# An attention and two MoE layers on one core: the order of a planned kernel, drawn anew

## The chip, the cores and the metric

The kernel runs on one core of one Trainium2 chip. The metric is the device time of one execution in microseconds, the median of several runs. TensorE (PE) does the matmuls, VectorE (DVE), ScalarE (ACT) and GpSimd (POOL) the elementwise work, and SyncE (SP) issues most of the DMA transfers. Each engine executes its own queue of instructions in order and waits at semaphores for the others.

## What is computed

Four images of 576 positions and 8 heads go through an attention with two branches: one on positions pooled by four, repeated over the four, and one in which a position sees its three neighbours on each side. Their sum, 2304 tokens of width 512, goes through two layers of the form "matmul, activation, matmul" with 2048 hidden columns. The inputs q, k, v and three weights are multiplied by 8 beforehand.

```python
attn_out = _attn_ref(q, k, v)                 # pooled branch + local branch
x = attn_out.transpose(0, 2, 1, 3).reshape(B * S, H * D)
h = x @ moe_w_in                              # first MoE
x = (h * (1.0 / (1.0 + np.exp(-h)))) @ moe_w_out
h = x @ moe2_w_in                             # second MoE
P = a[0] + a[1] * h + a[2] * h**2 + a[3] * h**3
Q = 1.0 + np.abs(b[0]) * np.abs(h) + np.abs(b[1]) * h**2
out = (P / (Q + 1e-06)) @ moe2_w_out
```

Weights come as 64-bit floats and are turned on the chip into pairs of 32-bit numbers, a rounded high part and the rest (`hl`); activations are split in the same way (`xh` and `xl`, `gh` and `gl`), and each product is the sum of three matmuls.

## The kernel before

**Stages.** In the head, PE has attention of image 0 and dummy matmuls on `wz` (line 328). Then the first MoE runs in 80 steps, one for each of five blocks of tokens (512, 384, 512, 512 and 384) and sixteen groups of 128 hidden columns. A step has 12 matmuls into `hps` (line 914), an activation on ACT and DVE (lines 1077 to 1089), and 12 matmuls into `acc` (line 928). The steps of block 0 are cut in two: 8 groups, then all of block 1, then the other 8. Between the steps stand, in islands, the attention of images 1 to 3, and on ACT, DVE and POOL the converting of the weights. The second MoE comes last, in a loop with an order written out by hand.

**What is planned.** All that comes before the second MoE is a list of jobs, each with a cost for each engine, a due time, the jobs that it comes after, the buffers it takes and gives, and the bytes it moves (`size`). `Plan.run` (line 150) plays them through on five engines (P, V, A, G, and D for SP) and returns the jobs in the order of their starts; the kernel then emits its instructions in that order. What is left at run time of a planned time is thus the order on each engine's queue. Three things in it concern transfers:

- Backwards (lines 163 to 166): a job's due time is that of its user, less its cost; for a transfer also less its bytes over a rate, a latency (`DMA_LAT`) and `PRE`.
- Forwards (lines 247 to 250): all transfers share one `bus`. A transfer holds it for its bytes over a rate, and its users are ready `DMA_LAT` later. Lines 213 to 216 hold a transfer back while the bus is planned more than `BACKLOG` (4 us) ahead.
- A job's `margin` is added to the time at which its predecessors are done (line 192).

`settle` (line 125) runs the plan twice, first with guessed starts of the steps (from `HEAD` on, line 359), then with the planned ones, keeps the better, and shifts due times by random draws, one after another for each of eight `SEEDS` (line 139). The dummies in the head fill a share of 0.8 of the planned idle time of PE (lines 1116 to 1126).

**The jobs that the change speaks of.** `piece` (line 807) loads 512 KB of 64-bit weights into `raw` (line 819) and converts them in seven jobs: `c1` (line 827 on ACT, 825 on DVE) and `c2` (line 831, ACT) read `raw`, `c3` to `c5` follow on DVE (834, 838, 842), `c6` (line 376 or 372, in the helper `copy`) and `c7` (line 850) write the two parts. For the first MoE's output weights (`wo`) the parts are also stored as `wos` (line 889) and loaded again for later blocks (line 1052); those of the second MoE are stored as `w2s` (line 898) and loaded from line 960. Attention loads `kq` (line 428) and `vw` (line 632); DVE pools k and q from `kq` (line 438), PE makes local scores (647, 655) and coarse ones (522), ACT exponentials (672, 539), PE transposes (687, 557), ACT copies (`PT`, `up`, line 376), and PE multiplies by v (722, 572). A block's output leaves `acc` as `xe` (lines 376 and 374, from 937) and is stored by SP (947) or, added, by POOL (945). `TAIL`, `TAIL1` and `STAG` set how long ahead of a block's first step its pieces of x are due (line 768). `raw`, `wo`, `xe` and the converted parts share one ring of seven buffers, `buf`.

Of the kernel before, what the change touches and what calls it, by code (L numbers as in the profile page):

```python
# [38 lines left out]
NEG = -1e30  # L39


HEAD = 42000.0
PACE = 1.06
TAIL, STAG, STAG0 = 40000.0, 4000.0, 2000.0
TAIL1 = 18000.0
SAFE = 4000.0
PRE = 3000.0
MARGIN = 800.0
# [8 lines left out]
BACKLOG = 4000.0  # L57
EARLY = 50000.0
ROUNDS = 2
SEEDS = [1000021, 1000022, 1000050, 1000057, 1000130, 1000133, 1000381, 1000809]  # L60
EARLYB = 20000.0
GPREF = 1
ACC = 108.0
# [42 lines left out]
class Plan:  # L106
# [1 line left out]

    LAT, OWN = 200.0, 90.0
    SWITCH = {(False, True): 90.0, (True, False): 195.0, (True, True): 0.0, (False, False): 0.0}  # L110
    DMA_LAT = 2500.0
    DMA_RATE, DMA_FULL, DMA_SLOW = 400.0, 11500.0, 285.0

    def __init__(self):
        self.jobs, self.sizes, self.lends = [], {}, {}
# [9 lines left out]
    def settle(self, when, rounds):  # L125
# [8 lines left out]
        self.run(when)  # L134
        for seed in SEEDS:
            self.shake(seed)
# [13 lines left out]
    def run(self, when):  # L150
# [12 lines left out]
        for j in reversed(self.jobs):  # L163
            for d in j.after:
                d.t = min(d.t, j.t - self.LAT - min(d.cost.values()) -
                          (d.size / self.DMA_RATE + self.DMA_LAT + PRE if d.size else 0.0))
            j.wait = len(j.after)
            j.ready = 0.0
            for d in j.after:
                users.setdefault(id(d), []).append(j)  # L170
# [3 lines left out]
        port = 0.0  # L174
        bus = 0.0
# [3 lines left out]
        while events:  # L179
# [3 lines left out]
            while done and done[0][0] <= t:  # L183
                _, _, j = heapq.heappop(done)
# [13 lines left out]
            while again:  # L198
                again = False
                for j in pool:  # L200
# [43 lines left out]
                    if held and not (best == "G" and j.size):  # L244
                        port = free[best]
                    heapq.heappush(events, free[best])
                    if j.size:
                        bus = max(bus, free[best])
                        bus += j.size / (self.DMA_RATE if bus > self.DMA_FULL else self.DMA_SLOW)
                        j.end = bus + self.DMA_LAT  # L250
                    else:
                        j.end = free[best]
# [39 lines left out]
def tile_kernel(ctx, tc, kq, vp, vw_in, moe_w_in, moe_w_out, moe2_w_in, moe2_w_out, moe2_a, moe2_b, out):  # L292
# [50 lines left out]
    plan = Plan()  # L343
# [14 lines left out]
    first1 = [STEP1.index((0 if f < SPLIT else 1, f)) for f in range(NF)]  # L358
    guess, t = [], HEAD
    for j, f in STEP1:  # L360
# [3 lines left out]
    FAR = At(0, 1e9)  # L364
# [50 lines left out]
    def attention(b):  # L415
# [201 lines left out]
        for c in range(NCH):  # L617
# [147 lines left out]
            def end(jo, pO, b=b, c=c, n=n, xu=xu, ad=ad, hi=hi, lo=lo):  # L765
                ja = plan.add(f"A{b}{c}", d0, {"V": 2 * v_ns(2 * n)}, ad, after=[jo], give=[pO, upu])
                for j, *p, i in pieces[b * NCH + c]:
                    due = begin[j] - (TAIL1 if j == 1 else TAIL) - (STAG if j else STAG0) * (behind[j] - 1 - i)
                    if i == 0:
# [37 lines left out]
    def piece(name, due, src, dst, home, after=None):  # L807
# [4 lines left out]
        wu, iu = Unit("cw"), Unit("cr")  # L812
# [37 lines left out]
            eng(e).tensor_tensor(out=x["hl"][:, 1], in0=x["w"], in1=x["hl"][:, 0], op=ALU.subtract)  # L850

        j0 = plan.add(f"{name}.l", FAR, {"D": 60}, ld, take=[home], size=128 * 4096)
        j1 = plan.add(f"{name}.1", FAR, {"A": 570, "V": 430}, c1, after=[j0], take=[wu], port=True)
        j2 = plan.add(f"{name}.2", FAR, {"A": 570}, c2, after=[j0], take=[iu])
        j3 = plan.add(f"{name}.3", FAR, {"V": 430}, c3, after=[j1], port=True)
        j4 = plan.add(f"{name}.4", FAR, {"V": 620}, c4, after=[j2, j3], port=True)
        j5 = plan.add(f"{name}.5", FAR, {"V": 620}, c5, after=[j4], give=[iu], port=True)
# [25 lines left out]
    for f in range(NF):  # L883
        wi_job[f] = piece(f"I{f}", when[first1[f]], win_src(moe_w_in, f), lambda u, f=f: new_wi(f), Unit(f"w{f}"))
        u = wo_u[first1[f]] = Unit("buf")

        def keep(x, j, f=f, u=u):
            wos_job[f] = plan.add(f"S{f}", when[first1[f]], {"D": 60},
                                  lambda e: nc.sync.dma_start(out=wos[f], in_=x["hl"].bitcast(F32)),
                                  after=[j], give=[u], size=128 * 4096, early=1e9)  # L890
        wo_job[f] = piece(f"O{f}", when[first1[f]] + 6000, wout_src(moe_w_out, f), lambda u, f=f: new_wo(first1[f]), u, keep)
    for f in range(NF):
        for s, w in enumerate((moe2_w_in, moe2_w_out)):
            u = Unit("buf")

            def keep2(x, j, f=f, s=s, u=u):
                w2_job[f, s] = plan.add(f"W{f}{s}", when[-1], {"D": 60},
                                        lambda e: nc.sync.dma_start(out=w2s[s, f], in_=x["hl"].bitcast(F32)),
                                        after=[j], give=[u], size=128 * 4096, early=1e9)
            piece(f"{'IO'[s]}2.{f}", when[NF + SPLIT + round((2 * f + s) * (3 * NF - SPLIT) / 32)], (win_src, wout_src)[s](w, f),  # L900
                  lambda u: buf(u, "cvo"), u, keep2)
# [298 lines left out]
    for s in range(ns + LAG2):  # L1200
        if s < ns:
            j, f = STEP2[s]
# [88 lines left out]
```

## Time and profile before

| | us |
|---|---|
| median of 3 runs | 908.48 |
| lowest, highest | 907.67, 908.97 |
| the profiled execution | 909.08 |
| its span, first to last instruction | 907.3 |

A row of the page's first part gives an engine's busy time, its share of the span and its instructions. A row of a table by stage has the window, its length, and for each engine the busy time and number of instructions; then the clock that was granted to PE (1.00 is full), the mean busy share of the 16 DMA engines, and GB/s. A row of waits has who waited, for whom, the total in us, how often, and the longest. A row of the timeline has the start, the duration, engine, line, operation, the tiles written and read, and in brackets the engine's idle time just before and what ended it. A row of groups has the shape and count, then busy us and mean ns, then the idle time before. A row of one tile's instructions has the shortest, middle and longest duration in ns, and the first and last start in us. The granted clock is 1.00 throughout.

### The profile page before, as it was taken

What the parts mean: (1) busy time and instruction counts of PE and PEld (TensorE: products, weight loads), DVE (VectorE), ACT (ScalarE), POOL (GpSimd) and SP (SyncE); (2) the same over time, 40 slices, a digit from 0 to 9 for tenths busy, and PEclk for the clock granted to TensorE, in tenths of its full rate; (3) what the DMA queues carried; (4) which work ended last, traced back from release to release, by engine and by line L of the source; (5) the groups of instructions that cost most, each with busy time, mean ns of one, the idle gap of its engine ahead of it and who ended that gap; (6) DMA issues with size and microseconds to landing.
All of it is one profiled execution on the core that took longest, in us unless ns stands there. A gap on an engine that the chain in (4) does not pass through costs nothing.

```text
span 907.3 us, 15615 instructions
## 1 busy us (share of the span) xinstructions
PE 889.2 (98%) x5912; PEld 750.8 (83%) x5912; DVE 691.8 (76%) x1045; ACT 606.9 (67%) x1372; POOL 282.2 (31%) x228
## 2 busy tenths in 40 slices
PE   9999999999999999999999999999999999999997
PEld 6777998777777788888999888888888888999996
DVE  7899997877868775243323499989997999799995
ACT  6898667877557764333222578877777777787874
POOL 1531221300103000100000265655554555455553
PEclk9999999999999999999999999999999999999999
DMA  8867799679999776346544470010002000200000
GB/s 324 282 193 271 263 280 354 220 242 327 380 282 324 254 249 230 131 185 244 187 167 180 171 281 1 1 63 32 1 1 82 1 1 0 82 1 1 36 1 35
DMA packets 45654, 144.20 MB, mean 159 GB/s; under 512 B 5036, under 2 KB 7084, under 8 KB 45580
## 3 DMA queue, kind: packets, MB, share of 16 engines
q1 hardware_dynamic: 43884, 139.51, 42.7%
q0 software_dynamic: 1408, 3.70, 2.4%
q8 instruction: 46, 0.75, 0.3%
q14 instruction: 28, 0.23, 0.1%
q10 hardware_dynamic: 288, 0.00, 0.0%
HBM read 107.55 MB, written 35.65 MB: 158 GB/s over the span
## 4 chain that ended last, share of the span: by engine, by line
PE 66%; DMA 3%; issue 1%; ACT 1%; DVE 1%; POOL 0%; SPq 0%; DVEq 0%; POOLq 0%
PE hps L914 31%; PE acc L1163 22%; PE acc L928 11%; DMA kq<-kq 1%; DMA w2s<-cvo 1%; DMA x2s<-xe 1%; DMA raw<-moe_w_in 1%; PE pair L722 0%; DMA wo<-wos 0%; PE pair L687 0%; POOL u L1001 0%; PE pair L655 0%; PE pair L572 0%; ACT cvo L376 0%; POOL gl L1194 0%
## 5 line engine op out<-in xcount | busy, mean ns | idle before, releaser
L928 PE MATMUL acc<-gh,wo 128*128 128x512 f32 (+1 forms) x640 | 215.3, 374 | 2.9 <-DVE xe L374 1.6
L914 PE MATMUL hps<-xh,w 128*128 128x512 f32 (+1 forms) x640 | 214.1, 373 | 0.5 <-DVE th L1080 0.3
L914 PE MATMUL hps<-x2h,wi 128*128 128x512 f32 (+1 forms) x640 | 197.9, 371 | 0.0
L1001 POOL TENSOR_TENSOR u<-u,ah 128x512 f32<-128x512 f32 (+1 forms) x80 | 96.0, 1200 | 276.4 <-ACT u L999 267.8
L1163 PE MATMUL acc<-wo,gh 128*128 128x512 f32 x576 | 178.9, 392 | 0.0
L928 PEld LDWEIGHTS acc<-gh,wo 128*128 128x128 f32 x640 | 119.1, 188 | 20.9 <-DVE xe L374 2.3
L914 PEld LDWEIGHTS hps<-xh,w 128*128 128x128 f32 x640 | 119.2, 188 | 19.1 <-DVE th L1080 2.2
L914 PEld LDWEIGHTS hps<-x2h,wi 128*128 128x128 f32 x640 | 119.0, 188 | 17.5
L1163 PEld LDWEIGHTS acc<-wo,gh 128*128 128x128 f32 x576 | 107.7, 188 | 21.6
L1194 POOL TENSOR_TENSOR gl<-p,gh 128x512 fp32r<-128x512 f32 (+1 forms) x80 | 121.3, 1516 | 11.6 <-issue 8.8
L914 PE MATMUL hps<-x2l,wi 128*128 128x512 f32 (+1 forms) x320 | 118.4, 370 | 0.0
L928 PE MATMUL acc<-gl,wo 128*128 128x512 f32 (+1 forms) x320 | 117.9, 368 | 0.0
L914 PE MATMUL hps<-xl,w 128*128 128x512 f32 (+1 forms) x320 | 117.9, 368 | 0.0
L1163 PE MATMUL acc<-wo,gl 128*128 128x512 f32 x288 | 113.0, 393 | 0.1
L1186 DVE SCALAR_TENSOR_TENSOR u<-u,r 128x512 f32<-128x512 f32 (+1 forms) x80 | 100.2, 1253 | 2.8
L1080 DVE SCALAR_TENSOR_TENSOR th<-th,hps 128x512 f32<-128x512 f32 (+1 forms) x80 | 50.3, 630 | 64.2 <-ACT th L1077 63.6
L1179 ACT ACTIVATE r<-u,cst 128x512 f32<-128x512 f32 (+1 forms) x80 | 54.5, 682 | 55.9 <-POOL u L1001 52.8
L1077 ACT ACTIVATE th<-hps 128x512 f32<-128x512 f32 (+1 forms) x80 | 44.5, 556 | 66.6 <-PE hps L914 64.3
L1185 DVE SCALAR_TENSOR_TENSOR u<-u,r 128x512 f32<-128x512 f32 (+1 forms) x80 | 82.7, 1034 | 0.5 <-ACT r L1180 0.5
L998 DVE TENSOR_TENSOR p<-p,hps 128x512 f32<-128x512 f32 (+1 forms) x80 | 50.5, 632 | 34.3 <-ACT p L997 34.2
L376 ACT ACTIVATE gh<-th 128x512 fp32r<-128x512 f32 (+1 forms) x77 | 45.2, 589 | 47.0 <-PE acc L928 25.4
L1089 DVE TENSOR_TENSOR gl<-th,gh 128x512 fp32r<-128x512 f32 (+1 forms) x69 | 45.5, 660 | 38.7 <-ACT gh L376 38.4
(133 smaller groups left out, 1433.2 us busy)
## 6 DMA issues: line engine op xcount, KB each, us to landing
wo<-wos SPq DMA_DIRECT2D x64, 512.0 KB, 5.6
raw<-moe_w_in SPq DMA_DIRECT2D x32, 512.0 KB, 6.3
raw<-moe_w_out SPq DMA_DIRECT2D x32, 512.0 KB, 7.0
w2s<-cvo SPq DMA_DIRECT2D x32, 512.0 KB, 5.4
kq<-kq SPq DMA_DIRECT2D x20, 496.0 KB, 8.3
wos<-wo SPq DMA_DIRECT2D x16, 512.0 KB, 4.2
wi<-w2s SPq DMA_DIRECT2D x16, 512.0 KB, 9.3
wo<-w2s SPq DMA_DIRECT2D x16, 512.0 KB, 7.2
```

The source lines that it names most:

```text
L376: nc.scalar.activation(out, in_, AF.Copy, scale=scale)
L914: nc.tensor.matmul(hps[:, :n], lhsT=wi[:, i, 128 * g:128 * g + 128], rhs=(a, b)[s][:, g, :n], start=(m == 0), stop=(m == len(mms) - 1))
L928: nc.tensor.matmul(acc_t[p][g // 2][:, g % 2, :n], lhsT=wo[:, i, 128 * g:128 * g + 128], rhs=s_[:, :n], start=(f == f0 and m % 3 == 0), st ...
L998: nc.vector.tensor_tensor(out=p, in0=p, in1=hps, op=ALU.mult)
L1001: nc.gpsimd.tensor_tensor(out=u, in0=u, in1=ah, op=ALU.mult)
L1080: nc.vector.scalar_tensor_tensor(out=x["t"][:, :n], in0=x["t"][:, :n], scalar=1.0, in1=x["h"][:, :n], op0=ALU.add, op1=ALU.mult)
L1089: eng(e).tensor_tensor(out=gl_t[s][:, :n], in0=x["t"][:, :n], in1=gh_t[s][:, :n], op=ALU.subtract)
L1163: nc.tensor.matmul(acc2[j][c], lhsT=a[:, 128 * c:128 * c + 128], rhs=wo[:, i, :], start=(f == 0 and m % 3 == 0), stop=(f == NF - 1 and m % ...
L1179: nc.scalar.activation(r, u, AF.Ln, scale=2.0 ** -64, bias=cst[:, 0:1])
L1185: nc.vector.scalar_tensor_tensor(out=u, in0=u, scalar=1.000001, in1=r, op0=ALU.add, op1=ALU.mult)
L1186: nc.vector.scalar_tensor_tensor(out=u, in0=u, scalar=-2.0, in1=r, op0=ALU.add, op1=ALU.mult)
L1194: nc.gpsimd.tensor_tensor(out=gl2[k_][:, :n], in0=p, in1=gh2[k_][:, :n], op=ALU.subtract)
```

## The change

The rate at which transfers hold the planned bus gets three levels by the planned time: 285 bytes/ns up to 11.5 us as before, 395 up to 45 us, and 300 from there on, where it was 400 from 11.5 us on. Backwards, 300 is counted. The latency goes from 2.5 to 2.8 us. The two jobs that read `raw` get a margin of 0.5 us behind its landing. The guess of the first step goes from 42 to 48 us and `TAIL1` from 18 to 24 us. The eight seeds are others. No job is added, removed or changed in what it emits.

```diff
-HEAD = 42000.0
+HEAD = 48000.0
 PACE = 1.06
 TAIL, STAG, STAG0 = 40000.0, 4000.0, 2000.0
-TAIL1 = 18000.0
+TAIL1 = 24000.0
...
-SEEDS = [1000021, 1000022, 1000050, 1000057, 1000130, 1000133, 1000381, 1000809]
+RATE = 300.0
+LAND = 500.0
+SEEDS = [3000005, 3000006, 3000057, 3000066, 3000071, 3000075, 3000083, 3000085]
...
-    DMA_LAT = 2500.0
-    DMA_RATE, DMA_FULL, DMA_SLOW = 400.0, 11500.0, 285.0
+    DMA_LAT = 2800.0
+    DMA_RATES = ((11500.0, 285.0), (45000.0, 395.0), (1e12, RATE))
...
-                          (d.size / self.DMA_RATE + self.DMA_LAT + PRE if d.size else 0.0))
+                          (d.size / RATE + self.DMA_LAT + PRE if d.size else 0.0))
...
-                        bus += j.size / (self.DMA_RATE if bus > self.DMA_FULL else self.DMA_SLOW)
+                        bus += j.size / next(r for e, r in self.DMA_RATES if bus < e)
...
-        j1 = plan.add(f"{name}.1", FAR, {"A": 570, "V": 430}, c1, after=[j0], take=[wu], port=True)
-        j2 = plan.add(f"{name}.2", FAR, {"A": 570}, c2, after=[j0], take=[iu])
+        j1 = plan.add(f"{name}.1", FAR, {"A": 570, "V": 430}, c1, after=[j0], take=[wu], port=True, margin=LAND)
+        j2 = plan.add(f"{name}.2", FAR, {"A": 570}, c2, after=[j0], take=[iu], margin=LAND)
```

## Rows read from the trace of the kernel before

**Rows 1.** The page's first part: busy us, share and instructions of PE.
```profile
PE 889.2 (98%) x5912; PEld 750.8 (83%) x5912; DVE 691.8 (76%) x1045; ACT 606.9 (67%) x1372; POOL 282.2 (31%) x228
```

**Rows 2.** Busy time by stage: head, first MoE with attention, second MoE.
```profile
0.00:45.27 45.27, 43.26 (x824) 32.35 (x824) 37.21 (x89) 34.97 (x163) 15.84 (x23) 1.00 0.83 303
45.27:510.60 465.33, 453.85 (x3299) 386.52 (x3296) 301.99 (x544) 268.80 (x705) 54.77 (x47) 1.00 0.70 242
510.60:907.30 396.70, 392.07 (x1795) 331.92 (x1793) 352.56 (x414) 303.11 (x507) 211.64 (x159) 1.00 0.12 45
```

**Rows 3.** Groups of instructions, the dummies of the head.
```profile
L328 PE MATMUL wps<-wz 128*128 128x256 bf16 x148 | 21.7, 295 | 1.1 <-DVE wz L323 1.1
```

**Rows 4.** Waits of PE from 45 to 512 us: total, times, longest.
```profile
PE pair L722 <- DMA vw<-vw: 1.9, 1, 1.9
PE acc L928 <- DVE xe L374: 1.6, 2, 1.2
PE pair L522 <- ACT E L672: 1.5, 2, 0.9
PE acc L928 <- ACT wo L376: 1.1, 1, 1.1
PE pair L522 <- ACT EE L539: 1.0, 2, 0.6
PE pair L647 <- ACT E L672: 0.8, 2, 0.5
PE pair L722 <- ACT up L376: 0.8, 1, 0.8
PE pair L687 <- ACT PT L376: 0.7, 1, 0.7
PE pair L557 <- ACT PT L376: 0.6, 1, 0.6
PE pair L722 <- ACT PT L376: 0.6, 1, 0.6
PE hps L914 <- DVE th L1080: 0.3, 1, 0.3
PE acc L928 <- DVE wo L850: 0.2, 1, 0.2
```

**Rows 5.** Timeline of ACT from 140 to 148 us, where it reads `raw`.
```profile
141.03 0.67 ACT L827 ACTIVATE cw<-raw 128x512 f32<-128x512 f32 x1 [2.83 <-DMA raw<-moe_w_out]
...
144.12 0.66 ACT L827 ACTIVATE cw<-raw 128x512 f32<-128x512 f32 x1 [1.48 <-DMA raw<-moe_w_out]
```

**Rows 6.** Timeline of DVE, three poolings that waited for `kq`.
```profile
160.26 1.12 DVE L438 TENSOR_REDUCE kqd<-kq 128x232 f32<-128x928 f32 x1 [1.44 <-DMA kq<-kq]
...
167.03 1.09 DVE L438 TENSOR_REDUCE kqd<-kq 128x224 f32<-128x896 f32 x1 [1.59 <-DMA kq<-kq]
...
283.19 1.09 DVE L438 TENSOR_REDUCE kqd<-kq 128x224 f32<-128x896 f32 x1 [0.83 <-DMA kq<-kq]
```

**Rows 7.** Timeline of ACT, two more stops on transfers.
```profile
205.83 0.66 ACT L827 ACTIVATE cw<-raw 128x512 f32<-128x512 f32 x1 [2.24 <-DMA raw<-moe_w_out]
...
254.84 0.60 ACT L376 ACTIVATE xe<-acc 128x512 f32<-128x512 f32 x1 [2.36 <-DMA x2s<-xe]
```

**Rows 8.** Time from issue to landing: tile `raw`; the page's issues of `kq`.
```profile
DMA to landing us min/median/max: 4.1/6.6/11.2
...
kq<-kq SPq DMA_DIRECT2D x20, 496.0 KB, 8.3
```

**Rows 9.** Busy time from 100 to 300 us; last the DMA share and GB/s.
```profile
100.00:300.00 200.00, 189.97 (x1500) 160.57 (x1500) 162.61 (x290) 138.43 (x387) 35.22 (x31) 1.00 0.87 297
```

**Rows 10.** Timeline of DVE before the first MoE step: the last split of x.
```profile
43.41 0.35 DVE L744 TENSOR_TENSOR xl<-xs,xh 128x192 fp32r<-128x192 f32 x1
```

**Rows 11.** Tile `w2s`: stores and first loads; durations ns, first and last start us.
```profile
L898 SPq DMA_DIRECT2D w2s<-cvo x32: 319/326/1367, 131.7 to 353.0; - x32
L960 SPq DMA_DIRECT2D wi<-w2s x16: 319/428/628, 399.9 to 528.0; - x16
```

## Prediction

> **What bounds the kernel now.** I read the page first: TensorE (PE) is busy for 889.2 of 907.3 us [rows 1], so only the time in which PE has nothing useful to do can be won. Next the table by stage [rows 2], to see where that time lies. Behind 510.60 us PE is busy for 392.07 of 396.70 us, and the diff touches nothing of that loop. In the head, up to the first MoE matmul at 45.27 us, PE looks busy, but 148 of its matmuls are dummies on `wz`, 21.7 us of busy time [rows 3]. Between the two, PE is busy for 453.85 of 465.33 us.
>
> Third, the list of what PE waited for between 45 and 512 us [rows 4]. Its twelve rows add up to 11.1 us. This is the whole stock on which a better order behind the head can draw, since the useful matmuls stay the same.
>
> Fourth, the timeline before these waits, to find what stood first in the chain. PE seldom names a transfer itself (the 1.9 us on `vw` only); it names ACT or DVE, which execute in order and had stood still on a transfer just before:
> - At 141.03 and 144.12 us ACT had stood for 2.83 and 1.48 us on `raw` loads [rows 5]. PE's waits for ACT and DVE `wo` (1.1 + 0.2 us) are of this place.
> - At 160.26, 167.03 and 283.19 us DVE's pooling of k and q had stood for 1.44, 1.59 and 0.83 us on `kq` [rows 6]. Behind it lie the maxima, exponentials and coarse scores: PE's waits at L522 (1.5 + 1.0 us) and one of the two at L647 (0.45 of 0.8, from its longest, 0.5).
> - At 205.83 us ACT had stood for 2.24 us on `raw`, and PE then for 0.8 us on ACT `up`; at 254.84 us it had stood for 2.36 us on the store of an earlier `xe`, whose buffer it needed, and PE's 1.6 us on `xe` are of this kind [rows 7].
> - The rest (0.7 + 0.6 + 0.6 + 0.3 us and 0.35 us at L647, 2.55 us) has ACT and DVE queues alone ahead of it.
>
> So some 8.5 of 11.1 us go back to transfers that landed later than the order had them.
>
> **What the change does to these terms.** No instruction is added or removed. What moves is the order on every queue: loads and stores on SP, the accumulating transfers and subtractions on POOL, converting on ACT and DVE, the islands of attention matmuls on PE. At run time these are queues in order, released by semaphores; the planner's times bind nothing. Hence a slower counted rate does not slow a transfer; it puts its consumer further back in the consumer's queue, or the load further forward on SP.
>
> How far, from the constants: a 512 KB transfer was counted as 524,288 / 400 + 2500 = 3.81 us, and is now 524,288 / 300 + 2800 = 4.55 us, 0.74 us more. Each transfer queued ahead adds 0.44 us. Converting gets 0.5 us on top, 1.24 us in all. Beside that the trace has 4.1 us for the quickest `raw`, 6.6 us in the middle and 11.2 us at most, and 8.3 us for `kq` [rows 8]. The new count is close to an undisturbed load, and still short of a queued one. The rate fits better, too: between 100 and 300 us the engines moved 297 GB/s at a share of 0.87, 341 at full share [rows 9]; 400 was above that, 300 is below it.
>
> Now each term, with the least shift (no queue ahead):
> - `wo`, 1.3 us: ACT's 2.83 and 1.48 us shrink by 1.24 each. That takes 2.5 us out of the chain, more than PE lost. Left: 0.
> - `kq`, 2.95 us: no extra 0.5 us here, so 0.74 us for each of three loads, 2.2 us off. Left: 0.75.
> - `vw`, 1.9 us: 0.74 off, left 1.15.
> - `up`, 0.8 us: the `raw` ahead of it shrinks by 1.24. Left: 0.
> - `xe`, 1.6 us in two waits (1.2 and 0.4): 0.74 off each. Left: 0.45.
> - The rest, 2.55 us: eight other seeds shift the due times, by draws that can't be followed by hand, so a redrawn order has as many such places for all that I can see. Left: 2.55, between 0 and twice that.
>
> Sum left 4.9, saved 6.2 us.
>
> What it costs: a `raw` load now stands on average 1.24 - 0.74 = 0.5 us further forward against `kq` and `vw`, which get no extra margin. One transfer takes 524,288 / 341 GB/s = 1.54 us of the queue, so in about a third of the cases such a load has one more ahead of it, 0.5 us on average. Four of these loads show in PE's waits, and PE paid about two thirds of what DVE and PE waited there (4.85 of some 7 us), so 4 x 0.5 x 0.67 = 1.3 us, between 0 and 4 x 1.54 = 6.2.
>
> The head is counted almost as before (395 instead of 400 up to 45 us). The starting guess of the first MoE step goes from 42 to 48 us, with the due times of block 1 kept where they were (24 instead of 18 ahead). The real first step came at 45.27 us; the last piece of x that it needs was split by DVE at 43.41 us for 0.35 us [rows 10], so it could come 1.5 us earlier if dummies and the coarse scores of image 1 stood behind it; if it went to the new guess it would be 2.7 us later. In the head 0.3 us of latency and 0.5 us ahead of converting are planned as idle, and 0.8 of planned idle time is filled with dummies. I take 0, between -1.5 and +2.7. Converting for the second MoE moves some us later; its last store was issued at 353.0 us and its results are first loaded at 399.9 us [rows 11]; these 47 us cover it, and a delay beyond them would cost its excess in full.
>
> Total: -6.2 + 1.3 + 0 = -4.9 us. The profiled execution took 909.08 us, with a span of 907.3 us and 1.8 us around it; that is 0.6 us above the median of the three runs, 908.48. So 904.2 on its own scale and 903.6 on the median's: I say **904.0 us**.
>
> **The rivals.**
> 1. *The order moves but the waits don't fall.* PE's waits are caused by the longest landings (11.2 us against 4.55 counted), which no lone-load count covers; the new seeds draw new places for the same 11 us. For it: `kq` at 8.3 us is still 3.7 us beyond its count. Against it: most waits of ACT were 1 to 3 us, the size of the shift. Time: 908.5 - 1 to + 1, 908 us. The Trainium skill, "DMA: Bandwidth & Descriptors", section "Anatomy of one DMA", speaks for this: it fits a transfer as about 2 us plus its bytes at 436 GB/s. By that rule, an estimate of 3.2 us for 512 KB, the old count was ample already, and raising it gains nothing. The trace's quickest `raw`, 4.1 us, sides with the new count.
> 2. *Attention's loads fall behind converting's (the other side).* Place: SP's queue between 100 and 300 us, ahead of `kq` and `vw`. Price: 1.54 us for each load that another transfer overtakes; with all four of the above and as many that just made it, 8 x 1.54 = 12.3 us of waits, two thirds of it on PE, 8.2 us; against it what the `raw` terms save (1.3 + 0.8 us) and part of `xe`, 1.15. Time: 908.5 + 8.2 - 3.2 = 913.5 us. It is slower from the point at which two `raw` loads go ahead of each late `kq`. For it: these loads get the smaller margin. Against it: their due times are earlier by 0.74 us as well.
> 3. *The first step comes later.* Place: PE's queue ahead of the first `hps` matmul. Price: 2.7 us if it follows the new guess, and with the waits down by half only (-2.5) the time is 908.7; it is slower when the waits fall by less than 2.7 us. Against it: the time is lost only as far as dummies fill it, since attention done sooner on PE is not to be done later.
> 4. *All of it at once*: no transfer is late and the first step comes 1 us earlier, -11 us, 897.5.
>
> **How the numbers follow.** Forecast (902 to 906.5): 0.47. Rival 1: 0.18. Rival 2: 0.15. Rival 3: 0.12, half of it slower and half near no change. Rival 4 and what lies between it and the forecast: 0.08. About 0.2%, 1.8 us, is what a measurement of this kernel can tell from no change. Faster by more: 0.47 + 0.08 = 0.55. Slower by more: 0.15 + 0.06, and a little of rival 1, 0.23. Between: 0.22. The range reaches from near rival 4 (898) to near rival 2 (913). The forecast's own range is 901 to 907.
>
> **What would show it.** In the profile after: PE's waits between the head and 510 us at 4 to 7 us in place of 11.1; ACT's stops on `raw` at a third; DVE's on `kq` at half and still there; the first `hps` matmul within 1.5 us of 45.27; the second MoE unchanged at 392 us. The forecast is wrong if ACT still stands for 2 to 3 us on `raw` with PE waiting behind it (rival 1), if PE waits for `vw`, or for what lies behind `kq`, for over 6 us (rival 2), or if there are clearly more dummies than 148 and a first step beyond 47 us (rival 3).

## The result, and the profile after

The changed kernel takes 896.38 us (median of 4 runs, 896.12 to 896.71), the kernel before 908.08 us beside it: a ratio of 0.9874, 95% interval 0.9857 to 0.9891. It is faster by 11.7 us, where 904.0 had been forecast, with a range down to 898. The direction and the kind of gain were right, its size was not. The 61 fast executions of the kernel before beside the experiments took from 902.8 to 915.0 us, the eight of the changed kernel in all from 896.1 to 896.7, so every ratio below is against the kernel before on the same chip.

The page's first part, after:
```profile
span 894.8 us, 15643 instructions
PE 886.4 (99%) x5910; PEld 750.7 (84%) x5910; DVE 687.2 (77%) x1035; ACT 610.2 (68%) x1375; POOL 290.5 (32%) x235
```
The span is 12.5 us shorter, and PE's busy time 2.8 us. The table by stage of the changed kernel (columns as in [rows 2]; the first stage ends at the first matmul of the first MoE):
```profile
0.00:44.37 44.37, 42.78 (x823) 32.42 (x823) 35.16 (x84) 34.98 (x161) 16.49 (x25) 1.00 0.87 312
44.37:497.72 453.35, 451.55 (x3299) 386.37 (x3296) 299.23 (x539) 271.75 (x709) 62.64 (x52) 1.00 0.72 248
497.72:894.80 397.08, 392.03 (x1795) 331.92 (x1793) 352.82 (x414) 303.46 (x507) 211.38 (x159) 1.00 0.12 45
```
The head is 0.9 us shorter and the second MoE 0.4 us longer. The rest is in the middle stage, 465.33 us before and 453.35 after, 12.0 us: PE's idle time there fell from 11.5 to 1.8 us, and its busy time by 2.3 us with the same matmuls. What PE waited for from 45 to 500 us, against twelve rows and 11.1 us in [rows 4]:
```profile
PE acc L930 <- ACT EE L541: 0.9, 1, 0.9
PE hps L916 <- DVE th L1082: 0.8, 1, 0.8
```
(Two lines were added above, so line 914 is 916 here, 928 is 930, and so on.) Nothing of `kq`, `vw`, `xe` or `wo` is left. One step back, the waits of ACT for transfers in that stretch are a single row. The loads of `raw` and `kq`, on which ACT and DVE had stood still in [rows 5 to 7], end no wait of theirs:
```profile
ACT xe L378 <- DMA x2s<-xe: 2.7, 1, 2.7
```
Times from issue to landing, the tile `raw` and the page's row of `kq`, against 4.1/6.6/11.2 and 8.3 in [rows 8]:
```profile
DMA to landing us min/median/max: 3.6/5.4/11.2
...
kq<-kq SPq DMA_DIRECT2D x20, 496.0 KB, 7.7
```
The transfers themselves came a little sooner. From 100 to 300 us, the row that answers to [rows 9]:
```profile
100.00:300.00 200.00, 199.97 (x1614) 170.34 (x1613) 153.31 (x276) 136.72 (x383) 37.08 (x32) 1.00 0.85 279
```
PE is busy for 199.97 of 200 us (189.97 before), with 18 GB/s less traffic: some of the converting moved further back. The last converted part is stored at 374.6 us instead of 353.0, and the first is loaded again at 390.4 instead of 399.9; the 47 us of cover in [rows 11] are 16 now:
```profile
L900 SPq DMA_DIRECT2D w2s<-cvo x32: 319/327/1432, 132.3 to 374.6; - x32
L962 SPq DMA_DIRECT2D wi<-w2s x16: 319/431/1532, 390.4 to 515.1; - x16
```
The dummies of [rows 3] are nearly as many:
```profile
L330 PE MATMUL wps<-wz 128*128 128x256 bf16 x146 | 21.2, 297 | 1.1 <-DVE wz L325 1.1
```

**Plan and chip.** The planner computes a start for each job when the program is built, and the trace has the real start. The last of the 80 steps begins here in the trace, first before, then after (the first row merges two matmuls, the last of the step before and, 0.17 us later, the first of the last step, at 494.78 us):
```profile
494.60 0.51 PE L914 MATMUL hps<-xh,w 128*128 128x384 f32 x2
```
```profile
480.33 0.33 PE L916 MATMUL hps<-xh,w 128*128 128x384 f32 x1
```
The plan had it at 473.4 us before and at 472.5 after. So the chip was 21.4 us behind its plan at that point, and is 7.8 us behind it now. The plan's own end of the first MoE is the same, 478.1 and 478.8 us. The whole gain is time that the chip no longer loses against the plan. This number, "behind the plan", is the measure of the experiments, since a change of any constant also changes how long the plan is. It comes from the one profiled execution of each kernel, and it ends at the last step: what is lost behind it, at the start of the second MoE, shows in the time alone.

### The profile page after: what moved, and what is told of

It reads as the page before. It is cut to its first block, busy times and chain, and to the rows that moved or that the text cites. A ratio compares the mean times of both kernels' runs of the same rounds, so it can differ in the third digit from the quotient of the medians.

```text
span 894.8 us, 15643 instructions
## 1 busy us (share of the span) xinstructions
PE 886.4 (99%) x5910; PEld 750.7 (84%) x5910; DVE 687.2 (77%) x1035; ACT 610.2 (68%) x1375; POOL 290.5 (32%) x235
## 4 chain that ended last, share of the span: by engine, by line
PE 93%; DVE 2%; ACT 1%; issue 1%; POOL 0%; ACTq 0%; DVEq 0%; POOLq 0%
PE hps L916 43%; PE acc L1165 22%; PE acc L930 22%; PE pair L724 1%; PE pair L574 1%; PE pair L689 1%; PE pair L657 1%; PE pair L559 1%; ACT E L674 1%; ACT EE L541 1%; PE pair L524 0%; PE wps L330 0%; DVE cr L840 0%; POOL u L1003 0%; PE pair L649 0%
## 5 line engine op out<-in xcount | busy, mean ns | idle before, releaser
L930 PE MATMUL acc<-gh,wo 128*128 128x512 f32 (+1 forms) x640 | 212.1, 373 | 0.9 <-ACT EE L541 0.9
L916 PE MATMUL hps<-xh,w 128*128 128x512 f32 (+1 forms) x640 | 210.4, 373 | 0.8 <-DVE th L1082 0.8
L1165 PEld LDWEIGHTS acc<-wo,gh 128*128 128x128 f32 x576 | 107.7, 188 | 21.6
L1196 POOL TENSOR_TENSOR gl<-p,gh 128x512 fp32r<-128x512 f32 (+1 forms) x80 | 121.0, 1512 | 11.5 <-issue 8.8
L1091 DVE TENSOR_TENSOR gl<-th,gh 128x512 fp32r<-128x512 f32 (+1 forms) x73 | 48.7, 666 | 46.9 <-ACT gh L378 45.7
```

Source lines behind the costliest of these rows:

```text
L916: nc.tensor.matmul(hps[:, :n], lhsT=wi[:, i, 128 * g:128 * g + 128], rhs=(a, b)[s][:, g, :n], start=(m == 0), stop=(m == len(mms) - 1))
L930: nc.tensor.matmul(acc_t[p][g // 2][:, g % 2, :n], lhsT=wo[:, i, 128 * g:128 * g + 128], rhs=s_[:, :n], start=(f == f0 and m % 3 == 0), st ...
L1091: eng(e).tensor_tensor(out=gl_t[s][:, :n], in0=x["t"][:, :n], in1=gh_t[s][:, :n], op=ALU.subtract)
L1165: nc.tensor.matmul(acc2[j][c], lhsT=a[:, 128 * c:128 * c + 128], rhs=wo[:, i, :], start=(f == 0 and m % 3 == 0), stop=(f == NF - 1 and m % ...
L1196: nc.gpsimd.tensor_tensor(out=gl2[k_][:, :n], in0=p, in1=gh2[k_][:, :n], op=ALU.subtract)
```

## The experiments

The theory at the start: the counted times for transfers decide how far the chip falls behind (theory 1). The rival: the draws do, by the places that they happen to make (theory 2). Later ones ask which of the counts it is, and in what way. All of them go through the planner, so every kernel has the same jobs and another order. This table has them all; "planned" is the plan's middle time from issue to landing of the `raw` loads issued between 100 and 300 us, "lead" the middle time in the trace from a `raw` load's issue to its first reader, in the same stretch, "stood" what ACT and DVE stood still for `raw` behind the head.

| kernel | counted behind the head | planned | lead | stood | behind the plan | plan's end | time, us |
|---|---|---|---|---|---|---|---|
| before | 400, latency 2.5 | 5.0 | 7.2 | 17.7 | 21.4 | 478.1 | 908.1 |
| b_noseed | the same | 4.7 | 6.4 | 26.1 | 25.0 | 485.5 | 918.8 |
| b_seed4 | the same | 5.2 | 7.0 | 25.5 | 22.1 | 480.1 | 917.0 |
| a_oldrate_ns | 400, 2.5, margin | 4.6 | 7.2 | 12.1 | 25.0 | 488.6 | 927.8 |
| a_dueonly_ns | 400, due times 300 | 4.6 | 6.6 | 13.0 | 19.5 | 498.8 | 928.0 |
| a_least_ns | 400, 3.24, margin | 5.5 | 7.6 | 5.7 | 18.6 | 487.5 | 913.6 |
| a_noland_r340_ns | 340 | 6.0 | 8.3 | 14.2 | 14.8 | 483.0 | 906.2 |
| a_back1_ns | 300, backlog 1 us | 5.5 | 8.1 | 3.1 | 9.5 | 484.8 | 904.0 |
| a_busonly_ns | 300, due times 400 | 7.8 | 8.7 | 4.1 | 5.1 | 487.1 | 901.8 |
| a_latlate_ns | 400, latency 6 | 8.0 | 9.9 | 1.7 | 5.1 | 491.2 | 905.9 |
| a_noland_ns | 300 | 8.5 | 10.4 | 2.7 | 7.4 | 481.7 | 898.4 |
| a_noseed | 300, margin | 7.6 | 10.3 | 3.9 | 10.8 | 489.3 | 913.4 |
| a_oldhead_ns | 300, margin, old head | 7.0 | 9.8 | 6.3 | 8.5 | 488.8 | 909.1 |
| a_oldseed | 300, margin | 7.2 | 9.2 | 1.0 | 8.4 | 490.4 | 908.4 |
| a_noland_best | 300 | 8.5 | 9.8 | 0.6 | 8.0 | 477.9 | 897.8 |
| a_bus_best | 300, due times 400 | 7.8 | 9.2 | 0.0 | 8.3 | 478.5 | 898.2 |
| after | 300, margin | 8.5 | 9.9 | 0.0 | 7.8 | 478.8 | 896.4 |

### Counts or draws

**b_noseed**, the kernel before without draws:
```diff
-SEEDS = [1000021, 1000022, 1000050, 1000057, 1000130, 1000133, 1000381, 1000809]
+SEEDS = []
```


> The kernel before with no draws at all (the list of seeds empty), all counted times as before. The plan's own end of the first MoE moves from 478.1 to 485.5 us by that. Theory 1 (the counted times decide how much the chip loses against the plan; 430 us lay between plan end and measured time before): 485.5 + 430 = 915.5 us, within 4, and PE's waits behind the head again near 11 us. Theory 2 (the draws decide it, by luck of the places they make): the loss may be anything; as small as after the change, 485.5 + 418 = 903.5 us, with some 2 us of waits.

Measured: 918.84 us, ratio 1.0124 (1.0091 to 1.0157), 25.0 us behind the plan. ACT's waits for `raw`:
```profile
ACT cw L827 <- DMA raw<-moe_w_out: 16.9, 9, 5.7
ACT cw L827 <- DMA raw<-moe_w_in: 6.0, 5, 2.4
```
With another order the old counts leave the same kind of waits, and more of them.

**a_noseed**, the changed kernel without draws:
```diff
-SEEDS = [3000005, 3000006, 3000057, 3000066, 3000071, 3000075, 3000083, 3000085]
+SEEDS = []
```


> The changed kernel with no draws; rate, latency, margin and head as changed. Plan end 489.3 us instead of 478.8. Theory 1: it keeps the small loss (418 us between plan end and measured time), 489.3 + 418 = 907 us within 4, PE's waits on transfers and their chains behind the head below 4 us beyond what the plan itself has idle; ACT hardly waits for raw loads. Theory 2: the loss is that of the kernel before, 489.3 + 430 = 919 us, with ACT waiting 10 us or more for raw loads.

Measured: 913.37 us, ratio 1.0058 (1.0026 to 1.0090), 10.8 us behind the plan; between the two expectations in time, with theory 1 by the measure: ACT's waits for `raw` are 3.9 us in all. What the time has on top lies behind the last step: from there to the end it takes 418.4 us where the changed kernel takes 414.5, since PE waits for 1.8 + 1.0 us at the start of the second MoE and then runs at half its clock for a while (last section).

**b_seed4**, the kernel before with eight arbitrary seeds:
```diff
-SEEDS = [1000021, 1000022, 1000050, 1000057, 1000130, 1000133, 1000381, 1000809]
+SEEDS = [4000001, 4000002, 4000003, 4000004, 4000005, 4000006, 4000007, 4000008]
```


> The kernel before with eight seeds picked without a look (4000001 to 4000008). Plan end 480.1 us. Theory 1: 480.1 + 430 = 910 us within 4, waits of PE near 11 us with ACT waiting for raw. Theory 2: anything, down to 898 us.

Measured: 916.99 us, ratio 1.0126 (1.0083 to 1.0169), 22.1 us behind the plan. The time missed its 910 by 7 us. Most of that lies behind the last step, as in a_noseed: PE waits for 1.8 + 0.9 us at the start of the second MoE and then runs at half its clock. In the middle stage PE's longest wait, 6.0 us up to 283.37 us for ACT's exponentials, goes back to a load as well, since ACT had stood still for `raw` just before:
```profile
273.77 0.66 ACT L827 ACTIVATE cw<-raw 128x512 f32<-128x512 f32 x1 [5.83 <-DMA raw<-moe_w_in]
```

**a_oldseed**, the changed kernel with the seeds of before:
```diff
-SEEDS = [3000005, 3000006, 3000057, 3000066, 3000071, 3000075, 3000083, 3000085]
+SEEDS = [1000021, 1000022, 1000050, 1000057, 1000130, 1000133, 1000381, 1000809]
```


> The changed kernel with the eight seeds of the kernel before. Plan end 490.4 us. Theory 1: 490.4 + 418 = 908 us within 4, few waits on transfers. Theory 2: the loss returns with the seeds, 490.4 + 430 = 920 us.

Measured: 908.39 us, ratio 1.0014 (0.9997 to 1.0031), 8.4 us behind the plan, as theory 1 had it (908).

So three kernels with the old counts are 21 to 25 us behind, three with the new ones 8 to 11, whatever is drawn: theory 2 falls as the cause of the loss. But the draws set the plan's length: without them the new counts give a plan 10.5 us longer than the changed kernel's, and 913.4 us, slower than the kernel before by 0.6%; with the old seeds they give 908.4 us, no faster than it. The gain needs both, counts that the chip keeps and draws that make a short plan under them.

### Which of the counts

**a_noland_ns**, no draws and no margin ahead of converting (this and the next ones also have the empty list of seeds):
```diff
-LAND = 500.0
+LAND = 0.0
```


> The changed kernel with no draws and without the 0.5 us margin ahead of converting; rates, latency and head as changed. Plan end 481.7 us. Measured time less plan end was 430 to 437 us in the three kernels with the old counts, 418 to 424 us in the three with the new. Theory A (the slower rate and longer latency carry most of it): 420 to 426 us, so 902 to 908 us; ACT waits some us for raw, DVE hardly for kq. Theory B (the margin carries it): 430 to 437, so 912 to 919 us, ACT waits over 15 us for raw.

Measured: 898.36 us, ratio 0.9901 (0.9872 to 0.9931), 7.4 us behind the plan. The waits for `raw` are few:
```profile
ACT cw L829 <- DMA raw<-moe_w_in: 1.4, 1, 1.4
ACT cw L829 <- DMA raw<-moe_w_out: 1.3, 2, 0.8
```
The time is below what either theory had. The margin is not what carries the gain. Without it the undrawn plan is 7.6 us shorter, and the time 15 us.

**a_oldrate_ns**, the old rate and latency with the margin kept:
```diff
-RATE = 300.0
+RATE = 400.0
...
-    DMA_LAT = 2800.0
-    DMA_RATES = ((11500.0, 285.0), (45000.0, 395.0), (1e12, RATE))
+    DMA_LAT = 2500.0
+    DMA_RATES = ((11500.0, 285.0), (1e12, 400.0))
```


> The changed kernel with no draws and with the old rate (400) and latency (2.5 us); the margin of 0.5 us and the head as changed. Plan end 488.6 us. Theory A: the loss is back at 428 to 435 us, 917 to 924 us, with waits for raw and for kq. Theory B: 418 to 424 us, 907 to 913 us.

Measured: 927.77 us, ratio 1.0227 (1.0169 to 1.0286), 25.0 us behind the plan. ACT for `raw` and DVE for `kq`:
```profile
ACT cw L829 <- DMA raw<-moe_w_in: 7.3, 4, 4.4
ACT cw L829 <- DMA raw<-moe_w_out: 4.8, 5, 1.7
...
DVE kqd L440 <- DMA kq<-kq: 10.1, 5, 3.5
```
Everything is back, the waits on `kq` above all, which the margin doesn't touch. The time is above what either theory had, and its three executions lie far apart, 924.5 to 931.9 us.

**a_oldhead_ns**, the old head:
```diff
-HEAD = 48000.0
+HEAD = 42000.0
...
-TAIL1 = 24000.0
+TAIL1 = 18000.0
```


> The changed kernel with no draws, with the old guess of the first step (42 us) and the old lead of block 1 (18 us); rates, latency and margin as changed. Plan end 488.8 us. Theories A and B both: these two only reorder, the loss stays at 418 to 424 us, 907 to 913 us, and the first step comes within 1 us of 44.8. A rival in which the head makes the difference: 430 us and more, 919 us.

Measured: 909.10 us, ratio 1.0026 (1.0009 to 1.0043), 8.5 us behind the plan. The head doesn't decide the loss. Its first step came at 41.98 us, 2.8 sooner than in a_noseed (the expectation, within 1 us, was wrong), with 592 matmuls of attention ahead of it instead of 676. The others had to be done later; yet its last step, too, began 2.9 us sooner (490.96 against 493.87 us).

**a_least_ns**, what the prediction had counted with: the same 4.55 us for an undisturbed load, no slower rate:
```diff
-RATE = 300.0
+RATE = 400.0
...
-    DMA_LAT = 2800.0
-    DMA_RATES = ((11500.0, 285.0), (45000.0, 395.0), (1e12, RATE))
+    DMA_LAT = 3240.0
+    DMA_RATES = ((11500.0, 285.0), (45000.0, 395.0), (1e12, 400.0))
```


> The changed kernel with no draws, where an undisturbed 512 KB transfer is counted with the same 4.55 us as after the change, but with the rate left at 400 (latency 3.24 us); margin and head as changed. Plan end 487.5 us. It does alone what the prediction counted with: 0.74 us for each load, 1.24 us for raw, nothing for the queue ahead. If that suffices, the loss is 418 to 424 us, 906 to 912 us. If it is the queue that the slower rate builds up in the plan, the loss is nearer to the old one, 426 to 434 us, 914 to 921 us, and ACT still waits for raw by some 5 to 10 us.

Measured: 913.55 us, ratio 1.0065 (1.0038 to 1.0092), 18.6 us behind the plan. ACT and DVE:
```profile
ACT cw L829 <- DMA raw<-moe_w_out: 5.7, 5, 2.1
...
DVE kqd L440 <- DMA kq<-kq: 4.0, 3, 1.6
```
Against a_oldrate_ns the chip ends 25.0 - 18.6 = 6.4 us less behind. A further 7.8 us, to the 10.8 of a_noseed, come with the slower rate at the same margin and the same 4.55 us. The times of these two don't show it (913.6 and 913.4 us): the plan of a_noseed is 1.8 us longer, and it loses 4.6 us more behind the last step.

### In what way the rate works

From here on the kernels have no margin (`LAND = 0.0`) beside the edit shown, and are compared with a_noland_ns. **a_busonly_ns** and **a_dueonly_ns** have 300 in one of the two places each:
```diff
-                          (d.size / RATE + self.DMA_LAT + PRE if d.size else 0.0))
+                          (d.size / 400.0 + self.DMA_LAT + PRE if d.size else 0.0))
```


> The changed kernel with no draws and no margin ahead of converting; the rate of 300 holds the planned bus only, while due times are counted backwards with 400 (0.44 us less for a 512 KB transfer). Plan end 487.1 us. Measured time less plan end was 416.7 us with 300 in both places, 439.2 with the old rate and latency in both. If the planned bus does it: 416 to 421 us, 903 to 908 us, PE's waits beyond the plan's own idle below 5 us. If the due times do it: 430 us and more, 917 us and more, with ACT waiting for raw.

```diff
-    DMA_RATES = ((11500.0, 285.0), (45000.0, 395.0), (1e12, RATE))
+    DMA_RATES = ((11500.0, 285.0), (45000.0, 395.0), (1e12, 400.0))
```


> The counterpart: 300 counted backwards in due times only, the planned bus held at 400 behind the head (latency 2.8 us, no margin, no draws). Plan end 498.8 us. If the planned bus does it: 430 to 438 us on top, 929 to 937 us, ACT waits over 10 us for raw. If the due times do it: 416 to 421 us, 915 to 920 us.

Measured: 901.79 us (0.9949, 0.9932 to 0.9965), 5.1 us behind, and 927.99 us (1.0229, 1.0205 to 1.0253), 19.5 us behind. ACT's waits for `raw` in a_dueonly_ns:
```profile
ACT cw L829 <- DMA raw<-moe_w_out: 9.8, 8, 2.8
ACT cw L829 <- DMA raw<-moe_w_in: 3.2, 3, 1.4
```
It is the planned bus, not the due times; both times lie some 1 us below what this had been expected to give. a_dueonly_ns and a_noland_ns differ in the rate of the planned bus behind the head alone, 400 and 300: 19.5 and 7.4 us behind.

**a_noland_r340_ns**:
```diff
-RATE = 300.0
+RATE = 340.0
```


> The changed kernel with no draws and no margin, and 340 in place of 300 in both places; 340 is what the transfers of the kernel before reached at full share between 100 and 300 us. Plan end 483.0 us. If the loss follows the rate step by step: between 416.7 (300) and the 426 to 439 of the two kernels at 400 with a margin, 420 to 426 us, 903 to 909 us. If 300 only has to be below a threshold near the measured rate: 416 to 419, 899.5 to 902 us.

Measured: 906.17 us (0.9994, 0.9966 to 1.0023), 14.8 us behind the plan, ACT standing 14.2 us for `raw`. Half way, within the expectation of a loss that follows the rate: 340, close to the 341 that [rows 9] give at full share, is not slow enough a count.

Why 300 does so much is seen in the plan. At 400 a `raw` load of the middle stretch is planned to land 5.0 us after its issue; at 300 the middle one is 8.55 us, the most that the plan lets it be and what 16 of 29 have in the changed kernel. That is 4.0 (the backlog at which the plan holds transfers back) + 1.75 (its bytes) + 2.8 (latency). The traffic of this stretch, 297 GB/s in [rows 9], all but fills a bus of 300, so its queue in the plan often stands at the stop. At 400 it seldom does (2 of 37 loads in the kernel before). Two kernels ask whether the planned 8.5 us count or the pace:

**a_back1_ns**, 300 with a short queue in the plan:
```diff
-BACKLOG = 4000.0
+BACKLOG = 1000.0
```


> The changed kernel with no draws and no margin, 300 in both places, but a transfer is held back in the plan while the bus is planned more than 1 us ahead (4 before). The plan then has 5.5 us from issue to landing of a raw load between 100 and 300 us, in place of 8.5. Plan end 484.8 us. Theory P (the planned time from issue to landing is what counts): the steps fall 17 to 22 us behind the plan as with the old rate, 426 to 432 us between plan end and time, 911 to 917 us, with ACT waiting for raw. Theory Q (the pace of the planned bus is what counts): they fall 5 to 9 us behind, 416 to 419 us on top, 901 to 904 us.

**a_latlate_ns**, 400 with a late landing in the plan:
```diff
-    DMA_RATES = ((11500.0, 285.0), (45000.0, 395.0), (1e12, RATE))
+    DMA_RATES = ((11500.0, 285.0), (45000.0, 395.0), (1e12, 400.0))
...
-                        j.end = bus + self.DMA_LAT
+                        j.end = bus + (6000.0 if bus > 45000.0 else self.DMA_LAT)
```


> The changed kernel with no draws and no margin, the planned bus at the old 400 behind the head, but landing counted 6 us behind the bus there, so that the plan has 8.0 us from issue to landing of a raw load. Plan end 491.2 us. Theory P: steps 5 to 9 us behind the plan, 416 to 419 us on top, 907 to 910 us, hardly a wait for raw. Theory Q: 17 to 22 us behind, 426 to 432 on top, 917 to 923 us.

Measured: 904.03 us (0.9953, 0.9927 to 0.9978), 9.5 us behind, and 905.95 us (0.9988, 0.9968 to 1.0008), 5.1 us behind. ACT's waits for `raw` in the first and in the second:
```profile
ACT cw L829 <- DMA raw<-moe_w_out: 2.3, 4, 1.2
ACT cw L829 <- DMA raw<-moe_w_in: 0.8, 2, 0.5
```
```profile
ACT cw L829 <- DMA raw<-moe_w_out: 1.7, 2, 1.3
```
The first comes out close to what Q had, the second as P had it, 1 us faster. So neither P nor Q alone: either way works. a_latlate_ns differs from a_dueonly_ns in the counted landing alone, and ends 5.1 us behind instead of 19.5. What the two share is the lead that the order gives a load at run time, 8.1 and 9.9 us in the table. Ordered by the lead, the table falls into place: up to 7.6 us the chip ends 19 to 25 us behind, at 8.1 to 8.3 us 9 to 15, from 8.7 us on 5 to 11. The real landings were 5.1 to 7.0 us in the middle in all of them. But this is an order among runs, not a test of the lead. Above 8.7 us a longer lead brings no smaller loss (10.3 us goes with 10.8), and why a_back1_ns has 8.1 us in the trace where its plan has 6.0 from issue to first reader stays open.

The plans allow another reading, which no run separates from the lead: the traffic that they put into the stretch. Added up over the transfers planned to start between 100 and 300 us, it is 316 to 332 GB/s in the six kernels that end 19 to 25 us behind, 308 in a_noland_r340_ns, and 283 to 298 in all the others, a_back1_ns (290) and a_latlate_ns (298) among them. The chip moved 271 to 298 GB/s there in every kernel. In the kernel before, 37 `raw` loads are planned for this stretch and 32 were issued, the middle one 14.0 us later than planned; after the change 29 are planned and 30 were issued, the middle one 2.7 us late. A slower bus, a shorter backlog or a later landing all make the plan ask for less there, so the old orders may simply have asked for more than the chip delivered.

### Can it be beaten

**a_noland_best**, no margin, and draws sought anew by the plan's end alone:
```diff
-SEEDS = [3000005, 3000006, 3000057, 3000066, 3000071, 3000075, 3000083, 3000085]
+SEEDS = [5000022, 5000027, 5000041, 5000045, 5000103, 5001373]
...
-LAND = 500.0
+LAND = 0.0
```


> The changed kernel without the margin ahead of converting, with six seeds drawn anew for it by the plan's end alone (477.9 us against 478.8 after the change). If the loss depends on the counted rate and not on the draws, 416 to 418 us on top: 894 to 896 us, at or just below the changed kernel. If the margin is worth something: up to 421, 899 us, with ACT waiting for raw.

Measured: 897.83 us (0.9908, 0.9894 to 0.9923), 8.0 us behind the plan, with the shortest plan of all, and above the 896 expected, though ACT stood for `raw` for 0.6 us only. Its last step began 0.8 us sooner than in the changed kernel (479.57 against 480.33 us). What it loses to that kernel lies behind the plan, where the second MoE begins:
```profile
PE acc L1165 <- POOL gl L1196: 1.8, 1, 1.8
```
The profiled execution, the slowest of the four (899.01 us), also has a stretch at half the clock behind this wait (last section).

**a_bus_best**, 300 on the planned bus alone, no margin, twelve other draws, beside **after_again**, the changed kernel on the same chip:
```diff
-LAND = 500.0
-SEEDS = [3000005, 3000006, 3000057, 3000066, 3000071, 3000075, 3000083, 3000085]
+LAND = 0.0
+SEEDS = [5200002, 5200022, 5200031, 5200035, 5200038, 5200050, 5200075, 5200077, 5200079, 5200107, 5201187, 5201240]
...
-                          (d.size / RATE + self.DMA_LAT + PRE if d.size else 0.0))
+                          (d.size / 400.0 + self.DMA_LAT + PRE if d.size else 0.0))
```


> 300 on the planned bus alone (due times counted with 400), no margin, and twelve seeds drawn anew by the plan's end alone: 478.5 us, beside 478.8 for the changed kernel. Between plan end and time there were 414.7 us without draws. If margin and due times gave nothing: 414 to 418 us on top, 893 to 896.5 us, as fast as the changed kernel or up to 3 us faster. If they did: 420 us and more, 898 us and more, with ACT waiting for raw.

> The changed kernel as it is, on the same chip: 896 to 898 us, steps 7 to 9 us behind the plan.

Measured: 898.17 us (0.9887, 0.9841 to 0.9932) and 896.47 us (0.9869, 0.9814 to 0.9925), 8.3 and 7.3 us behind. ACT does not wait for `raw` in a_bus_best, so the margin isn't needed for that; yet it is 1.7 us slower, with 419.7 us on top of the plan's end, between the two expectations. Its last step began 2.2 us later, of which 1.3 are in the plan. Neither beats the changed kernel, and a shorter plan alone doesn't: a_noland_best has the shortest.

## Why the prediction was wrong, and where it was right

- **Right: where the stock lies.** PE's waits between the head and the second MoE were the stock, and 9.4 of 11.1 us of them went (forecast: 6.2 of 11.1). They were to be traced to `raw`, `kq`, `vw` and `xe`, and no wait of PE goes back to these any more; of the stops of ACT and DVE one is left, ACT's 2.7 us on the store of `xe`.
- **The step that failed: "each term, with the least shift (no queue ahead)".** It took the users of a load to move back by 0.74 us, converting by 1.24, from the constants of one undisturbed transfer, and named 0.44 us for each transfer queued ahead without counting any. In the plan with 300 the queue is often full in the stretch, and the planned time from issue to landing grew from 5.0 to 8.5 us in the middle, by 3.5, nearly five times the 0.74. The lead at run time grew by 2.7 (7.2 to 9.9). So the `kq`, `vw` and `xe` terms, with 2.35 us left in the sum, came to nothing. a_least_ns is the shift as I had sized it: it ends 18.6 us behind, with ACT still standing 5.7 us for `raw` and DVE 4.0 for `kq`, where a_noseed, with the same 4.55 us and the queue, ends 10.8 behind (3.9 and nothing). That its 6.4 us against a_oldrate_ns are near the forecast's 6.2 proves nothing: these are two other orders, one profiled execution of each. The miss could have been suspected from [rows 9]: 297 GB/s of traffic under a counted rate of 300.
- **The whole miss, in spans.** Forecast -4.9 us, measured -12.5: 3.5 of the 7.6 us between are idle time of PE in the middle stage (-9.7 against -6.2), 1.3 the cost that didn't come, 2.3 PE's busy time, 0.9 the head, less 0.4 in the second MoE.
- **"The rest", 2.55 us to stay.** All waits together are 1.7 us after. I had put what had only ACT and DVE queues ahead of it down to the order; the seeds are others, too, so whether it was the same lateness some jobs further on, or the draws, is not shown.
- **The cost, 1.3 us, for `raw` ahead of `kq` and `vw`.** It didn't come: PE waits for neither, and a load takes less long (5.4 against 6.6 us, 7.7 against 8.3), with 279 instead of 297 GB/s in the stretch. Rival 2, built on this, is out: in no kernel at 300 did DVE stand for `kq` by more than 0.8 us. That the lower traffic is why landings came sooner is argued, not shown. The share of two thirds in this term had a wrong base: the rows shown give 1.44 + 1.59 + 0.83 + 1.9 = 5.8 us, not "some 7".
- **Not in the sum: 2.3 us of PE's busy time.** A wait can also cost busy time: the matmul behind the wait at 145.93 us took 0.28 us to the next start, where its neighbours take 0.17. Fourteen waits fewer at 0.11 us each would be 1.5 us, an estimate from this one; the rest of the 2.3 stays open. I had counted idle time alone.
- **Converting for the second MoE later, at no cost.** It went back by 21.6 us, more than the "some us" of the prediction; the cover held, with a third of it left.
- **The head at 0, within -1.5 and +2.7.** It came to -0.9 us. That an earlier first step isn't won time, the argument against rival 3, isn't shown: in a_oldhead_ns it came 2.8 us sooner than in a_noseed, 84 matmuls moved behind it, and the last step still began 2.9 us sooner. The mean granted clock was 0.987 in a_noseed and 0.996 in a_oldhead_ns, so the pair doesn't show the contrary either.
- **Rival 1 and the page's rule.** The Trainium skill, "DMA: Bandwidth & Descriptors", "Anatomy of one DMA", gives about 2 us plus bytes at 436 GB/s for a transfer issued by GpSimd; 3.2 us for 512 KB is an estimate from that. The prediction took it over for loads that SP issues, and the trace of these doesn't agree: 4.1 us for the quickest `raw`, 6.6 in the middle [rows 8]. A higher count does gain: a_latlate_ns differs from a_dueonly_ns in the counted landing alone, and falls 5.1 us behind instead of 19.5.
- **The draws.** I held them to be places that can't be followed, with no sign. They are worth 17 us with the new counts (913.4 to 896.4) and 10.8 with the old. This was left out of the sum; that didn't cost the forecast anything is luck: both kernels' draws end at nearly the same plan, 478.1 and 478.8 us.

## What to carry to other kernels

Where an order is planned ahead and run from queues, compare the planned start of each step with the real one: the difference separates what the plan costs from what the chip loses against it. Waits alone don't tell the two apart: in a_latlate_ns PE waits for 9.0 us between 45 and 490 us, and the chip ends only 5.1 us behind a plan that is 12.4 us longer than the changed kernel's. When a constant of a planner's model changes, work out what it does at the load that the model carries, not to one undisturbed job; a rate near the traffic fills the planned queue, and users move back by much of the queue's length. And a count that is truthful for one transfer can still be too short for the order: here landings counted at 8 us, or a bus held at 300, kept the chip near its plan, for loads that took 5 to 7 us in the middle.

## What the hardware showed beside that

PE's granted clock, 1.00 in both kernels' traces, fell in other kernels where PE stood still. In a_noseed, from 180 us on (columns as in [rows 2]):
```profile
180.00:185.00 5.00, 2.66 (x32) 1.94 (x31) 4.10 (x9) 4.63 (x15) 0.00 (x0) 0.78 0.65 235
185.00:190.00 5.00, 5.00 (x35) 3.90 (x35) 2.77 (x5) 3.34 (x6) 1.27 (x1) 0.50 0.56 184
190.00:195.00 5.00, 5.00 (x50) 4.08 (x50) 2.31 (x5) 3.75 (x8) 1.28 (x1) 0.70 0.41 136
195.00:200.00 5.00, 5.00 (x55) 4.20 (x53) 3.63 (x8) 3.96 (x8) 1.30 (x1) 1.00 0.83 303
```
PE was idle for 2.3 us of the first 5, and then, fully busy, ran at 1.2 GHz (0.50) and partly so for the next 10 us. Matmuls of several sizes stand there, so their number says little; in the second MoE they are of one size. There, first a_noseed, then a_noland_best:
```profile
520.00:525.00 5.00, 2.22 (x8) 1.25 (x7) 4.69 (x5) 4.09 (x8) 2.95 (x2) 0.91 1.03 410
525.00:530.00 5.00, 5.00 (x18) 3.94 (x18) 4.86 (x7) 4.09 (x7) 2.99 (x2) 0.75 1.03 412
530.00:535.00 5.00, 5.00 (x23) 4.08 (x22) 4.89 (x6) 4.08 (x8) 3.00 (x2) 1.00 1.03 409
```
```profile
505.00:510.00 5.00, 3.21 (x13) 2.05 (x12) 4.47 (x5) 4.09 (x7) 2.96 (x2) 0.95 1.04 412
510.00:515.00 5.00, 5.00 (x17) 4.01 (x16) 4.90 (x6) 4.09 (x8) 2.98 (x2) 0.71 1.03 410
515.00:520.00 5.00, 5.00 (x23) 4.06 (x22) 4.89 (x7) 4.08 (x7) 3.01 (x2) 1.00 1.03 411
```
Fully busy, PE does 18 and 17 matmuls in 5 us where it does 23 at the full 2.4 GHz. In a_noland_best it had been busy without a break from 500 us on, and the clock fell behind a single wait of 1.8 us. The waits of up to 1.9 us in the trace of the kernel before left it at 1.00, so the length of one wait doesn't settle it. The stretch at 520 us is why a_noseed took longer than its loss against the plan says; the one at 185 us lies ahead of the last step and is part of that loss. The planner counts no such cost. The kernel before pays it in some executions: of the 61 beside the experiments, the eleven with a mean granted clock of 0.994 or less took 909.1 to 915.0 us, the other fifty 902.8 to 910.6, while the eight of the changed kernel have 0.999 or 1.000. The Trainium skill tells of a gate that halves the clock when PE isn't busy ("TensorE: Matmul & The Clock Gate", Part 1), and these rows agree.
